# Stage one of a Fourier-mixing kernel: partner rows brought together through DRAM and added on GpSimd

## The chip, the cores and the metric

One core of a Trainium2 chip. The time is device microseconds of one execution of the whole program. Engines are named as the profile names them: PE (TensorE, matrix products; PEld is its weight load), DVE (VectorE), ACT (ScalarE), POOL (GpSimd) and SP (SyncE, which here issues DMA transfers). Sixteen DMA engines move data between DRAM and on-chip memory.

## The reference

```
x: (8, 3072, 256) float32, w1, w2, w3: (256, 768), w_out: (768, 256)
X   = real(fft(fft(x, axis=1), axis=2))         # per batch, 3072 x 256
t   = X.reshape(24576, 256)
h   = max(max(t @ w1, t @ w2), t @ w3)
out = h @ w_out                                  # (24576, 256) float32
```

## The kernel before

The two Fourier transforms are done as matrix products, and the product with w1, w2 and w3 is folded into the second transform's matrices (`gE`, `gO`, `gD`), so that the feed-forward part reads only two half-spectra `tE` and `tO` per batch.

A sequence of 3072 rows is written as 24 x 128, and the 256 columns as four groups `g` of 64. In on-chip memory a batch stands as 96 partitions (4 groups times 24 rows `a`), with 128 rows `bb` and 64 columns `dl` along the free dimension. x is loaded in four chunks `ch` of 32 rows `bb` (33 for the overlap) into tiles `xs` of 96 x 33 x 64 fp32: `load_chunk` (L123) issues on SP's queue four transfers of 24 partitions each (`load_rows`, L107), in pieces of 256 bytes, and for the last chunk five small ones of the row that follows (`load_next`, L119).

Since x is real, column d of a batch pairs with column 64 - d of another group, with reversed rows. `turn_chunk` (L144) on GpSimd therefore writes two bf16 copies of each batch from 1 on into `x0`: a forward one, transposed to d-major (L155), and a reversed one (`reverse`, L158). Batches 2 to 7 have each chunk in four parts, two forward and two reversed. Stage one, `Mix.s(k, x0)` (L487), takes five columns d per call (three in the last). For each d it runs two matmuls into one PSUM region, the forward copy by `m24f` (L496) and the reversed one by `m24r` (L498). A call's result is evicted to `z` by ACT (L503, L506, L507). Stage two, `Mix.k(q)` (L522, L524), multiplies `z` by the table `tabs` into `t`.

The feed-forward part of a batch has three blocks of six units, 18 units (`UNITS`) in all. A unit runs `unit_plus` (L542, L543), `unit_out` (a relu on ACT, L556, and a max on DVE, L557) and the `unit_minus` (L550) of the unit before, and then some steps of the output part (`l2_some`), taken from a queue. Per block there are four output lines ("slots"), twelve per batch. A slot goes through these engines:

- `l2_odd`: PE L591 into a bank `po` (two of them), DVE L594 (`other`), then POOL L597, which adds `even` and `other`;
- twelve matmuls of `l2_hidden` (PE L567) into the same bank;
- `l2_block`: DVE L617 adds `po` and the line that L597 completed, into `ot` (six buffers); POOL L620 stores half of it with an indirect DMA, and SP L630 the other half.

All engines run in the order in which the program was written down; nothing is reordered. That order is laid out by hand in `plan`: `at(b, unit, fn)` puts a step of work behind the given unit of batch b. Stage one and two of batch b + 1 go in from unit `begin[b]` on: `s0` to `s6`, then `k0` to `k5`. `turn_chunk` of batch b + 2 goes into units 6 to 21 of batch b (11 to 21 in batch 0), one part a unit, and the loads (`fetch`, L775) of batch b + 3 go into units 18, 19, 20 and 22 of batch b. Before the loop, a first section builds the tables and takes batch 0 through stage one.

Of the kernel before, what the change touches and what calls it, by code (L numbers as in the profile page):

```python
# [33 lines left out]
def kernel(  # L34
# [9 lines left out]
    nc = tc.nc  # L44

    B, S, D = x.shape
    assert (S, D) == (3072, 256)
    DFF = moe_w1.shape[1]
# [3 lines left out]
    UNITS = 3 * NJC  # L52
# [7 lines left out]
    consts = ctx.enter_context(tc.tile_pool(name="consts", bufs=1))  # L60
    ps_f = ctx.enter_context(tc.tile_pool(name="ps_f", bufs=2, space=bass.MemoryType.PSUM))
    xs_pool = ctx.enter_context(tc.tile_pool(name="xs", bufs=4))
    x0_pool = ctx.enter_context(tc.tile_pool(name="x0", bufs=2))
    t_pool = ctx.enter_context(tc.tile_pool(name="tbuf", bufs=2))

    m24f = consts.tile([96, 96], BF16, tag="m24f")
# [68 lines left out]
    def reverse(copy, xr, xs, r0, n, d0=32, d1=65):  # L135

        last = r0 + n > 128
        for (lo, hi, m) in ((d0, min(d1, 64), n), (64, d1, n - 1)) if last else ((d0, d1, n),):
            if lo < hi:
                copy(out=xr[:, lo - 32:hi - 32, 129 - r0 - m:129 - r0],  # L140
                     in_=bass.AP(xs.tensor, xs.offset + (m - 1) * 64 + lo,
                                 [xs.ap[0], [1, hi - lo], [-64, m]]))

    def turn_chunk(b, ch, part=None):  # L144

        if (b, "v") not in turned:
            x0 = x0_pool.tile([96, 66 * 130], BF16, name="x0", tag="x0")
            v = x0.rearrange("p (dl bb) -> p dl bb", bb=130)
            turned[b] = (lambda d: v[:, d, 0:128], rows_back(v[:, 33:66, :]))
            turned[b, "v"] = v  # L150
        v = turned[b, "v"]
        xs = raw[b, ch]
        for (d0, d1) in (((0, 17), (17, 33))[part % 2:part % 2 + 1] if part is not None else ((0, 33),)):
            if part is None or part < 2:
                nc.gpsimd.tensor_copy(v[:, d0:d1, ch * 32:ch * 32 + 32],  # L155
                                      xs[:, 0:32 * 64].rearrange("p (bb dl) -> p dl bb", dl=64)[:, d0:d1, :])
            if part is None or part >= 2:
                reverse(lambda out, in_: nc.gpsimd.tensor_copy(out, in_), v[:, 33:66, :], xs,  # L158
                        ch * 32, 33 if ch == 3 else 32, 32 + d0, 32 + d1)

    def signed():
        nc.scalar.activation(out=gw[:, 514:770], in_=gw[:, 256:512], func=AX.Copy, scale=sgn)
# [17 lines left out]
    def rows_back(v):  # L180
        return lambda d: v[:, 32 - d, 0:128] if d else v[:, 32, 1:129]

    raw_w = [consts.tile([128, 2 * DFF], FP32, name=f"raw_w{i}", tag=f"raw_w{i}") for i in (2, 3)]

    def cols(t, jh):
        return t.rearrange("p (fc j) -> p fc j", fc=2)[:, :, jh * 384:(jh + 1) * 384]
# [12 lines left out]
        nc.gpsimd.iota(t, pattern, base=base, channel_multiplier=cm,  # L199
                       allow_small_or_imprecise_dtypes=True)  # L200

    x0_first = x0_pool.tile([96, 64 * 130], BF16, name="x0", tag="x0")
    x0v = x0_first.rearrange("p (bb dl) -> p bb dl", dl=64)
    xs_a = xs_pool.tile([96, 33 * 64], FP32, name="xs", tag="xs")
    rows_a = xs_a.rearrange("p (bb dl) -> p bb dl", dl=64)
    load_rows((nc.sync, nc.sync, nc.scalar, nc.scalar), rows_a[:, 0:16, :], 0, 112, 128)
# [56 lines left out]
    turn = 2.0 * math.pi  # L263
# [34 lines left out]
    for (r0, r1) in ((0, 3), (3, 7)):  # L298
# [5 lines left out]
                          in_=up[:, 0:13].unsqueeze(1).to_broadcast([96, 2, 13]))  # L304
# [105 lines left out]
    for ch in range(4):  # L410
# [11 lines left out]
                        in_=moe_w_out.rearrange("(jc p) c -> p jc c", jc=NJC))  # L422
# [56 lines left out]
    class Mix:  # L479
# [7 lines left out]
        def s(self, k, x0, pool=ps_f, evict=nc.scalar.copy):  # L487

            ps1 = pool.tile([128, 512], FP32, name="ps1", tag="ps")
            if k < len(DLS):  # L490
                parts = [(d, 96, m24f, m24r) for d in range(*DLS[k])]
            else:
                parts = [(0, 52, m0f, m0r), (32, 48, m24f, m24r), (1, 96, m24f, m24r)]
            c0 = 0
            for (d, n, mf, mr) in parts:
                nc.tensor.matmul(ps1[:, c0:c0 + n], x0[0](d), mf[:, 0:n],  # L496
                                 start=True, stop=False)
                nc.tensor.matmul(ps1[:, c0:c0 + n], x0[1](d), mr[:, 0:n],  # L498
                                 start=False, stop=True)
                c0 += n  # L500
            if k < len(DLS):
                lo = 4 * DLS[k][0]
                evict(out=z[:, lo:lo + 20, 0:24],  # L503
                      in_=ps1[:, 0:480].rearrange("p (c r) -> p c r", r=24))
            else:
                evict(out=z_all[:, 0:52], in_=ps1[:, 0:52])  # L506
                evict(out=z[:, 2:8, 0:24],  # L507
                      in_=ps1[:, 52:196].rearrange("p (c r) -> p c r", r=24))
# [266 lines left out]
    def fetch(b, ch):  # L775
        raw[b, ch] = load_chunk(b, ch)
# [1 line left out]
    ahead = (("s0",), ("s1",), ("s2",), ("s3",), ("s4",), ("s5",), ("s6",),  # L778
             ("k0",), ("k1",), ("k2",), ("k3",), ("k4",), ("k5", "end"))
    first_ahead = (11, 12, 13, 13, 14, 14, 15, 16, 16, 17, 18, 19, 20)  # L780
    begin = [11, 6] + [5] * (B - 3)

    def l2_first():
        for _ in l2_even(0, 0):
# [3 lines left out]
    for (u, fn) in ((0, prep_some), (0, prep_some), (0, lambda: tab_sines(7, 10, (2,))),  # L788
                    (1, prep_some), (1, prep_some), (1, prep_some),
                    (2, lambda: m.k(2)), (2, prep_some), (2, lambda: tab_sines(10, 13, (0,))),  # L790
                    (3, prep_some), (3, lambda: tab_sines(10, 13, (1, 2))),
                    (4, lambda: m.k(3)), (4, prep_some), (5, prep_some), (5, l2_first),
                    (6, lambda: m.k(4)), (7, lambda: m.k(5)), (7, m.end),
                    (0, lambda: turn_chunk(1, 0)), (2, lambda: tab_minus(10, 13, nc.gpsimd)),
                    (2, lambda: turn_chunk(1, 1)),
                    (5, lambda: turn_chunk(1, 2)),
                    (7, lambda: turn_last(0)), (8, lambda: turn_last(1)),
                    (8, lambda: lay_last(0)), (9, lambda: lay_last(1)), (20, signed)):
        at(0, u, fn)
    for ch in range(4):  # L800
        at(0, (6, 7, 9, 11)[ch], lambda ch=ch: fetch(2, ch))
    for b in range(B - 1):
        for i, whats in enumerate(ahead):
            for what in whats:
                at(b, begin[b] + i if b else first_ahead[i], lambda b=b, what=what: piece(b + 1, what))
        if b + 2 < B:
            for ch in range(4):
                for part in range(4):
                    at(b, 6 + 4 * ch + part if b else 11 + 11 * (4 * ch + part) // 16,
                       lambda b=b, ch=ch, part=part: turn_chunk(b + 2, ch, part))  # L810
                if b + 3 < B:
                    at(b, UNITS + (0, 1, 2, 4 if b else 6)[ch], lambda b=b, ch=ch: fetch(b + 3, ch))

    for b in range(B):
        mm = mixes[b]
# [76 lines left out]
```

## Time and profile before

| | |
|---|---|
| median of 3 runs | 412.85 us (412.58 to 413.83) |
| the profiled execution | 412.57 us, its span 410.8 us |
| TensorE clock granted | 1.0 in all slices |
| PE busy | 393.8 us, 3018 matmuls |
| POOL busy | 319.8 us |
| DMA | 52.70 MB, mean 128 GB/s |

How to read it: the profile is of one execution. A group line names the source line, engine, operation, tiles with shape and type, count, then busy time, mean duration in ns and the idle time in front of it with what ended it. Queue q1 in the page's list is SP's DMA queue, q0 that of GpSimd. The "chain" follows the work that ended last back to the start.

### The profile page before, as it was taken

The page shows a single profiled execution, that of the slowest core. Times are in us where ns is not written, and L with a number is a line of the kernel's source. Part 1 is how long each engine was busy: PE and PEld are TensorE (multiplying, and loading weights), DVE is VectorE, ACT ScalarE, POOL GpSimd, SP SyncE. Part 2 cuts the span into 40 slices and gives each one's busy share as a digit, 9 for nine tenths or more (in the row PEclk, how much of TensorE's full clock was granted, in tenths as well). Part 3 has the DMA queues.
Part 4 walks back from the last instruction along what each step waited for, and adds up shares of the span by engine and source line. Part 5 has one row for each costly group of instructions (what it writes and reads, how often), then busy time and mean ns, then how long its engine had stood idle before and what let it go on. Part 6 is the DMA issues. An engine that isn't in the chain of part 4 may idle for free.

```text
span 410.8 us, 9043 instructions
## 1 busy us (share of the span) xinstructions
PE 393.8 (96%) x3018; PEld 268.9 (65%) x3072; DVE 308.8 (75%) x556; ACT 266.6 (65%) x489; POOL 319.8 (78%) x428
## 2 busy tenths in 40 slices
PE   0999999999999999999999999999999999999996
PEld 0465667766676677667676667667666666766665
DVE  8798767776768776786777777787668767778884
ACT  6787776767666667657765666656775676655550
POOL 9598999998888888889789798888878844446651
PEclk9999999999999999999999999999999999999999
DMA  9989895784228841586217852387411221211314
GB/s 116 194 173 180 179 234 148 183 205 111 81 87 207 172 136 53 140 211 141 100 65 188 190 137 88 94 208 151 124 65 67 65 76 67 79 53 51 107 65 142
DMA packets 131111, 52.70 MB, mean 128 GB/s; under 512 B 113009, under 2 KB 128120, under 8 KB 131064
## 3 DMA queue, kind: packets, MB, share of 16 engines
q1 hardware_dynamic: 106496, 37.50, 37.4%
q0 software_dynamic: 23632, 14.29, 15.7%
q8 instruction: 24, 0.39, 0.4%
q10 hardware_dynamic: 936, 0.33, 0.3%
q14 instruction: 23, 0.19, 0.2%
HBM read 29.02 MB, written 25.17 MB: 132 GB/s over the span
## 4 chain that ended last, share of the span: by engine, by line
PE 92%; POOL 3%; DVE 2%; issue 1%; DMA 1%; ACT 0%; DVEq 0%; ACTq 0%; POOLq 0%
PE po L567 31%; PE pse L542 16%; PE pse L550 15%; PE pse L543 13%; PE po L591 3%; PE ps L496 3%; PE ps L522 3%; POOL x L107 3%; PE ps L498 3%; PE ps L524 3%; PE pl L580 2%; DMA x<-in_x_dram 1%; PE psg L436 1%; DVE hm L557 1%; PE psw L465 0%
## 5 line engine op out<-in xcount | busy, mean ns | idle before, releaser
L556 ACT ACTIVATE stmp<-pse 128x512 bf16<-128x512 f32 x288 | 171.5, 600 | 44.9 <-PE pse L543 31.2
L557 DVE TENSOR_TENSOR hp<-pse,stmp 128x512 bf16<-128x512 f32 x144 | 99.4, 691 | 87.2 <-ACT stmp L556 64.5
L620 POOL DMA_INDIRECT out_dram<-ot,rows_m x92 | 102.6, 1115 | 53.2 <-DVE ot L617 41.3
L542 PE MATMUL pse<-t,gE 128*128 128x512 bf16 x288 | 109.2, 379 | 2.2
L557 DVE TENSOR_TENSOR hm<-pse,stmp 128x512 bf16<-128x512 f32 x144 | 99.1, 688 | 3.8 <-ACT stmp L556 3.5
L543 PE MATMUL pse<-t,gO 128*128 128x512 bf16 x249 | 94.3, 379 | 0.0
L567 PE MATMUL po<-wout_bf,hp 128*128 128x256 bf16 x576 | 85.9, 273 | 0.0
L567 PE MATMUL po<-wout_bf,hm 128*128 128x256 bf16 x570 | 85.3, 273 | 0.1
L597 POOL TENSOR_TENSOR even<-even,other 128x256 f32<-128x256 f32 x92 | 66.4, 722 | 21.9 <-DVE other L594 19.6
L550 PE MATMUL pse<-t,gD 128*128 128x512 bf16 x273 | 82.4, 379 | 0.7
L567 PEld LDWEIGHTS <-hp 128*128 128x128 bf16 x576 | 56.3, 98 | 17.1 <-issue 1.9
L567 PEld LDWEIGHTS <-hm 128*128 128x128 bf16 x576 | 56.3, 98 | 16.6
L617 DVE TENSOR_TENSOR ot<-po,even 128x512 f32<-128x512 f32 x92 | 62.7, 681 | 0.0
L158 POOL CAST x<-xs 96x544 bf16<-96x544 f32 (+5 forms) x57 | 60.5, 1068 | 0.0
L155 POOL CAST x<-xs 96x544 bf16<-96x544 f32 (+2 forms) x51 | 58.8, 1156 | 1.4 <-DMA xs<-in_x_dram 1.4
L526 ACT CAST t<-ps 128x512 bf16<-128x512 f32 x48 | 27.9, 585 | 34.5 <-PE ps L524 34.4
L550 PEld LDWEIGHTS <-gD 128*128 128x128 bf16 x288 | 27.9, 98 | 32.2
L503 ACT CAST z_all<-ps 128x480 bf16<-128x480 f32 x46 | 25.4, 559 | 33.5 <-PE ps L498 33.5
L594 DVE SCALAR_TENSOR_TENSOR other<-twice,po 128x256 f32<-128x256 f32 x92 | 43.7, 475 | 0.1
L543 PEld LDWEIGHTS <-gO 128*128 128x128 bf16 x288 | 28.1, 98 | 20.3 <-issue 2.0
L542 PEld LDWEIGHTS <-gE 128*128 128x128 bf16 x288 | 28.1, 98 | 19.6 <-issue 0.7
L583 ACT COPY even<-pl 128x512 f32<-128x512 f32 x46 | 27.0, 587 | 10.1 <-PE pl L580 9.7
(171 smaller groups left out, 382.9 us busy)
## 6 DMA issues: line engine op xcount, KB each, us to landing
xs<-in_x_dram SPq DMA_DIRECT2D x84, 198.0 KB
out_dram<-ot SPq DMA_DIRECT2D x90, 128.0 KB
xs<-in_x_dram SPq DMA_DIRECT2D x28, 192.0 KB
raw_w<-in_moe_w_dram SPq DMA_DIRECT2D x4, 384.0 KB
out_dram<-ot,rows_m POOLq DMA_INDIRECT x92, 3.6
out_dram<-ot SPq DMA_DIRECT2D x17, 64.0 KB
x<-in_x_dram POOLq DMA_DIRECT2D x8, 120.0 KB, 6.3
xs<-in_x_dram SPq DMA_DIRECT2D x32, 5.8 KB
```

Source lines behind the costliest of these rows:

```text
L155: nc.gpsimd.tensor_copy(v[:, d0:d1, ch * 32:ch * 32 + 32], xs[:, 0:32 * 64].rearrange("p (bb dl) -> p dl bb", dl=64)[:, d0:d1, :])
L158: reverse(lambda out, in_: nc.gpsimd.tensor_copy(out, in_), v[:, 33:66, :], xs, ch * 32, 33 if ch == 3 else 32, 32 + d0, 32 + d1)
L542: nc.tensor.matmul(pse[:, 0:n], gE[i][:, js], te, start=True, stop=False)
L543: nc.tensor.matmul(pse[:, 0:n], gO[i][:, js], to, start=False, stop=True)
L550: nc.tensor.matmul(pse, gD[i][:, js], to, start=False, stop=True, skip_group_check=True)
L556: nc.scalar.activation(out=stmp[:, 0:n], in_=pses[0][:, 0:n], func=AX.Relu)
L557: nc.vector.tensor_tensor(out=dst, in0=src3, in1=stmp[:, 0:n], op=ALU.max)
L567: nc.tensor.matmul(po, hcols(jc), wout_bf[:, jc * 256:(jc + 1) * 256], start=False, stop=(jc == NJC - 1), skip_group_check=True)
L594: nc.vector.scalar_tensor_tensor(out=other, in0=twice, scalar=po[:, 256:257], in1=po[:, 0:256], op0=ALU.mult, op1=ALU.subtract)
L597: nc.gpsimd.tensor_tensor(out=line[:, 256:512], in0=line[:, 0:256], in1=other, op=ALU.add)
L617: nc.vector.tensor_tensor(out=ot, in0=po, in1=lin, op=ALU.add)
L620: stored(nc.gpsimd.indirect_dma_start(out, bass.IndirectOffsetOnAxis(ap=rows_m[0:128 - lo, b * 12 + slot: b * 12 + slot + 1], axis=0), ot[ ...
```

## The change

For batches 2 to 7 the two bf16 copies are replaced by one folded copy `xw` of 34 x 128. Each chunk `xs` is sent as it is, fp32, to a DRAM buffer `held`, with the four groups in reversed order (`send_chunk`, four transfers of 24 partitions with 8,448 bytes in each), and read back from there into `xp` with the 24 rows of each group in reversed order (`fetch_turned`, one transfer of 96 partitions). So `xp` has in each partition the rows that pair with those of `xs`. `fold_chunk` adds the two on GpSimd in fp32, reading `xp` reversed, for d = 1 to 32 (in two parts of 16 columns), and writes bf16. Two small copies per chunk fill the columns 0 and 33. `Mix.s` then runs one matmul by `m24f` for each d from 1 to 32, and two for d = 0. Batches 0 and 1 stay as they were.

Chunks are taken in pairs, (1, 2) and (0, 3), since chunk `ch` needs the partner of chunk `3 - ch`. The loads come in the order 1, 2, 0, 3, from units 18, 19, 21 and 23. In batch b from 1 on, the first pair of batch b + 2 is sent at units 6 and 7, fetched at 8 and 9 and added at 10 to 13; the second is sent at 9 and 10, fetched at 14 and 15 and added at 16 to 19. Stage one of batch 2 begins at unit 8 of batch 1, and no longer at 6. To make room, `x0` has one buffer, and the fp32 weights `raw_w` share the two buffers of `xp`.

```diff
-    x0_pool = ctx.enter_context(tc.tile_pool(name="x0", bufs=2))
+    x0_pool = ctx.enter_context(tc.tile_pool(name="x0", bufs=1))
+    xp_pool = ctx.enter_context(tc.tile_pool(name="xp", bufs=2))
+    xw_pool = ctx.enter_context(tc.tile_pool(name="xw", bufs=2))
+    turn_pool = ctx.enter_context(tc.tile_pool(name="turn", bufs=4, space=bass.MemoryType.DRAM))
...
+    def send_chunk(b, ch):
+        xs = raw[b, ch]
+        held = turn_pool.tile([4, 24 * 33 * 64], FP32, name="held", tag="held")
+        for g in range(4):
+            nc.sync.dma_start(out=held[3 - g].rearrange("(a r) -> a r", a=24),
+                              in_=xs[g * 24:(g + 1) * 24])
+        sent[b, ch] = held
+
+    def fetch_turned(b, ch):
+        held = sent[b, ch]
+        xp = xp_pool.tile([128, 33 * 64], FP32, name="xp", tag="xp")[0:96]
+        n = 33 * 64
+        nc.sync.dma_start(out=xp, in_=bass.AP(held.tensor, held.offset + 23 * n,
+                                              [[24 * n, 4], [-n, 24], [1, n]]))
+        partner[b, ch] = xp
+
+    def fold_chunk(b, ch, part):
+        if b not in turned:
+            xw = xw_pool.tile([96, 34 * 128 + 16], BF16, name="xw", tag="xw")
+            turned[b] = xw[:, 0:34 * 128].rearrange("p (dl bb) -> p dl bb", bb=128)
+        v = turned[b]
+        bb = slice(ch * 32, ch * 32 + 32)
+        xs, xo, xp = raw[b, ch], raw[b, 3 - ch], partner[b, 3 - ch]
+        d0, d1 = ((1, 17), (17, 33))[part]
+        nc.gpsimd.tensor_tensor(
+            out=v[:, d0:d1, bb],
+            in0=xs[:, 0:32 * 64].rearrange("p (bb dl) -> p dl bb", dl=64)[:, d0:d1, :],
+            in1=bass.AP(xp.tensor, xp.offset + 33 * 64 - d0, [xp.ap[0], [-1, d1 - d0], [-64, 32]]),
+            op=ALU.add)
+        if part:
+            nc.gpsimd.tensor_copy(v[:, 33, bb], bass.AP(xo.tensor, xo.offset + 32 * 64,
+                                                        [xo.ap[0], [-64, 32]]))
+        else:
+            nc.gpsimd.tensor_copy(v[:, 0, bb], xs[:, 0:32 * 64:64])
...
-    raw_w = [consts.tile([128, 2 * DFF], FP32, name=f"raw_w{i}", tag=f"raw_w{i}") for i in (2, 3)]
+    raw_w = [xp_pool.tile([128, 33 * 64], FP32, name="xp", tag="xp")[:, 0:2 * DFF] for i in (2, 3)]
...
             for (d, n, mf, mr) in parts:
-                nc.tensor.matmul(ps1[:, c0:c0 + n], x0[0](d), mf[:, 0:n],
-                                 start=True, stop=False)
-                nc.tensor.matmul(ps1[:, c0:c0 + n], x0[1](d), mr[:, 0:n],
-                                 start=False, stop=True)
+                if isinstance(x0, tuple):
+                    pairs = ((x0[0](d), mf), (x0[1](d), mr))
+                else:
+                    pairs = ((x0[:, d, :], mf),) if d else ((x0[:, 0, :], mf), (x0[:, 33, :], mr))
+                for i, (st, mv) in enumerate(pairs):
+                    nc.tensor.matmul(ps1[:, c0:c0 + n], st, mv[:, 0:n], start=(i == 0),
+                                     stop=(i == len(pairs) - 1))
...
-    begin = [11, 6] + [5] * (B - 3)
+    begin = [11, 8] + [5] * (B - 3)
...
         if b + 2 < B:
-            for ch in range(4):
-                for part in range(4):
-                    at(b, 6 + 4 * ch + part if b else 11 + 11 * (4 * ch + part) // 16,
-                       lambda b=b, ch=ch, part=part: turn_chunk(b + 2, ch, part))
+            for pair, out_at, back_at, fold_at in (
+                    ((1, 2), *(((6, 7), (8, 9), (10, 11, 12, 13)) if b else
+                               ((11, 12), (13, 13), (15, 16, 17, 17)))),
+                    ((0, 3), *(((9, 10), (14, 15), (16, 17, 18, 19)) if b else
+                               ((14, 15), (17, 18), (20, 21, 22, 22))))):
+                for i in range(4):
+                    at(b, fold_at[i], lambda b=b, ch=pair[i % 2], part=i // 2:
+                       fold_chunk(b + 2, ch, part))
+                for i in range(2):
+                    at(b, out_at[i], lambda b=b, ch=pair[i]: send_chunk(b + 2, ch))
+                    at(b, back_at[i], lambda b=b, ch=pair[i]: fetch_turned(b + 2, ch))
```

More of the change, by code (lines that the diff above doesn't have):

```diff
@@ L142, in reverse, with turn_chunk @@
                                  [xs.ap[0], [1, hi - lo], [-64, m]]))
-    def turn_chunk(b, ch, part=None):
+    def turn_chunk(b, ch):
         if (b, "v") not in turned:
-            x0 = x0_pool.tile([96, 66 * 130], BF16, name="x0", tag="x0")
-            v = x0.rearrange("p (dl bb) -> p dl bb", bb=130)
+            x0 = x0_pool.tile([96, 68 * 128], BF16, name="x0", tag="x0")
+            v = x0[:, 0:66 * 130].rearrange("p (dl bb) -> p dl bb", bb=130)
             turned[b] = (lambda d: v[:, d, 0:128], rows_back(v[:, 33:66, :]))
@@ L152, in turn_chunk @@
         xs = raw[b, ch]
[L153 to L159, printed above, removed]
+        nc.gpsimd.tensor_copy(v[:, 0:33, ch * 32:ch * 32 + 32],
+                              xs[:, 0:32 * 64].rearrange("p (bb dl) -> p dl bb", dl=64)[:, 0:33, :])
@@ new lines, in turn_chunk @@
+        reverse(lambda out, in_: nc.gpsimd.tensor_copy(out, in_), v[:, 33:66, :], xs,
+                ch * 32, 33 if ch == 3 else 32)
+    sent = {}
+    partner = {}
+    def send_chunk(b, ch):
[12 more added lines that the diff above has]
+        partner[b, ch] = xp
@@ L200, in iota @@
                        allow_small_or_imprecise_dtypes=True)
-    x0_first = x0_pool.tile([96, 64 * 130], BF16, name="x0", tag="x0")
-    x0v = x0_first.rearrange("p (bb dl) -> p bb dl", dl=64)
+    x0_first = x0_pool.tile([96, 68 * 128], BF16, name="x0", tag="x0")
+    x0v = x0_first[:, 0:64 * 128].rearrange("p (bb dl) -> p bb dl", dl=64)
     xs_a = xs_pool.tile([96, 33 * 64], FP32, name="xs", tag="xs")
@@ L800 @@
     for ch in range(4):
-        at(0, (6, 7, 9, 11)[ch], lambda ch=ch: fetch(2, ch))
+        at(0, (6, 7, 9, 11)[ch], lambda ch=ch: fetch(2, (1, 2, 0, 3)[ch]))
     for b in range(B - 1):
@@ L806 @@
         if b + 2 < B:
-            for ch in range(4):
-                for part in range(4):
-                    at(b, 6 + 4 * ch + part if b else 11 + 11 * (4 * ch + part) // 16,
-                       lambda b=b, ch=ch, part=part: turn_chunk(b + 2, ch, part))
-                if b + 3 < B:
-                    at(b, UNITS + (0, 1, 2, 4 if b else 6)[ch], lambda b=b, ch=ch: fetch(b + 3, ch))
+            for pair, out_at, back_at, fold_at in (
[9 more added lines that the diff above has]
+                    at(b, back_at[i], lambda b=b, ch=pair[i]: fetch_turned(b + 2, ch))
+            if b + 3 < B:
+                for ch in range(4):
+                    at(b, UNITS + ((0, 1, 3, 5) if b else (0, 1, 5, 6))[ch],
+                       lambda b=b, ch=ch: fetch(b + 3, (1, 2, 0, 3)[ch]))
     for b in range(B):
```

## The prediction

> **What bounds the kernel now.** I read the page first, then the windows of steady batches, then TensorE's groups and one stretch of its timeline, then GpSimd against VectorE, and the DMA queues last. Page, busy times and chain:
>
> ```profile
> PE 393.8 (96%) x3018; PEld 268.9 (65%) x3072; DVE 308.8 (75%) x556; ACT 266.6 (65%) x489; POOL 319.8 (78%) x428
> PE 92%; POOL 3%; DVE 2%; issue 1%; DMA 1%; ACT 0%; DVEq 0%; ACTq 0%; POOLq 0%
> ```
>
> TensorE carries 92% of the chain. Three whole batches, from one first eviction of stage one to the next (columns: stretch, length, busy time and count by engine, clock, DMA share of 16 engines, GB/s):
>
> ```profile
> 134.60:181.80 47.20, 46.83 (x364) 32.50 (x370) 35.41 (x61) 31.01 (x57) 40.09 (x53) 1.00 0.53 136
> 181.80:229.00 47.20, 46.83 (x364) 32.38 (x369) 35.29 (x61) 31.01 (x57) 40.03 (x53) 1.00 0.52 136
> 229.00:276.20 47.20, 46.83 (x367) 32.45 (x371) 35.41 (x61) 30.96 (x57) 40.05 (x53) 1.00 0.54 137
> ```
>
> A batch is 47.20 us, 99% of it TensorE; a unit, its eighteenth, is 2.62 us. What is taken off TensorE comes off the time, as long as nothing else takes over the period. GpSimd (40.1) and the DMA engines (0.53 x 16 x 47.2 = 400 engine-us) have room on average. The 0.53 is not even, as the stretch with x loads shows beside the one after it (same columns):
>
> ```profile
> 169.00:188.00 19.00, 18.89 (x147) 12.72 (x147) 15.04 (x26) 11.67 (x21) 16.42 (x23) 1.00 0.89 206
> 188.00:216.00 28.00, 27.79 (x218) 19.57 (x221) 20.17 (x35) 19.10 (x37) 23.37 (x32) 1.00 0.29 91
> ```
>
> **TensorE's saving.** Timeline of one `s` piece, ten matmuls:
>
> ```profile
> 53.31 0.21 PE L496 MATMUL ps<-m24f,x 96*128 96x96 bf16 x1
> 53.36 0.20 PE L498 MATMUL ps<-m24r,x 96*128 96x96 bf16 x1
> ...
> 53.74 0.38 PE L542 MATMUL pse<-t,gE 128*128 128x512 bf16 x1
> ```
>
> Ten take 53.74 - 53.31 = 0.43 us, 0.043 each (0.2 is latency). The change drops 32 of 66 per batch (one each for d = 1 to 32): 32 x 0.043 = 1.4 us, a little less for the one of 48 columns; call it 1.35, and for six batches 8.1 us. The profiled execution took 412.57 us (span 410.8), the median of the runs is 412.85; so TensorE alone would give 412.6 - 8.1 = 404.5.
>
> **GpSimd.** Rows by form:
>
> ```profile
> L155 POOL CAST x<-xs 96x544 bf16<-96x544 f32 x24 | 27.2, 1133 | 0.0
> L155 POOL CAST x<-xs 96x512 bf16<-96x512 f32 x24 | 25.7, 1073 | 0.0
> L597 POOL TENSOR_TENSOR even<-even,other 128x256 f32<-128x256 f32 x92 | 66.4, 722 | 21.9 <-DVE other L594 19.6 <-ACT z_all L507 2.2
> L158 POOL CAST x<-xs 96x32 bf16<-96x32 f32 x6 | 1.4, 227 | 0.0
> ```
>
> Removed: 16 casts a batch, with L158's other forms (27.2 + 25.7 + 20.7 + 19.5 + 7.0 + 6.3 + 1.4)/6 = 18.0 us. Added: eight adds of 512 and eight copies of 32. An add is bounded below by the contiguous adds (256 in 0.722, 384 at L281 in 1.005, so 512 in 1.29) and above by two strided reads at the casts' 2 ns an element, 2.1; with the copies at 0.23, 12.2 to 18.6 us. GpSimd's sum stays or falls: nothing on the path by itself. But each add now waits for a DMA, and behind it in GpSimd's order stand L597 and the indirect store L620.
>
> **What those waits do.** A pair's fetches are put at units 8 and 9 (second pair 14, 15), and SP holds them back to back. The first add needs the second fetch, and is put at unit 10 (16), 2.6 us later. Cover on GpSimd and VectorE:
>
> ```profile
> 209.60 0.72 POOL L597 TENSOR_TENSOR even<-even,other 128x256 f32<-128x256 f32 x1
> 214.57 0.68 DVE L617 TENSOR_TENSOR ot<-po,even 128x512 f32<-128x512 f32 x1
> ```
>
> L597 at 209.60 serves the L617 at 214.57, and follows a cast directly; so a held add has some 4.3 us before L617 stands, and VectorE with it, and 1 to 2 more until TensorE has no free `pse` bank: 6 us in all.
>
> **DMA, the disputed cost.** Queues and sizes of before:
>
> ```profile
> q1 hardware_dynamic: 106496, 37.50, 37.4%
> q0 software_dynamic: 23632, 14.29, 15.7%
> xs<-in_x_dram SPq DMA_DIRECT2D x84, 198.0 KB
> out_dram<-ot,rows_m POOLq DMA_INDIRECT x92, 3.6
> ```
>
> From the trace's packet records, mean time: 256 B 19.4 ns, 1 KB 48.8, 4 KB 172, 8 KB (instruction fetch) 429 median and 307 at least. A row of 8,448 B is then 317 to 442 ns; I take 330, by the quick 8 KB ones and the 4 KB rate (355).
>
> How many engines share a transfer? q1's transfers move 89,568 rows of 256 B, 12,679 of 1 KB and 1,024 of 1.5 KB: 103,271. The other 3,225 packets are the 4-byte end marks, one for each engine used. They come out exactly with 16 marks for transfers of 128 or 64 rows (111 of them), 12 for 24 rows (114), 4 for 4 rows (8), 1 for 23 rows (32), 9 and 8 for the two odd stores: 1,776 + 1,368 + 32 + 32 + 17. So a transfer uses the largest number up to 16 that divides its rows. In all of these both sides count alike. The fetch does not: 96 partitions, from a pattern of 4 groups of 24 rows. Bounds: 16 engines by its target, 4 by its source's outer count. I take 4, nearest to the 4-row transfers, since 4 is the count that both sides can be cut by. Which four no view names; I take the same four each time, and price the rest as a rival.
>
> The Trainium skill, page "DMA: Bandwidth & Descriptors", section "Why a DMA increments its semaphore by 16 and not by 1", has a rule that speaks against this change: a transfer issued from SP takes the largest number of engines up to 16 that divides the slowest count of both sides, the lowest-numbered ones. By that rule the sum is the 555 below, and without it 434; the trace agrees for equal counts by the 3,225 marks, and no run so far shows unequal ones.
>
> On four engines a fetch is 24 rows x 0.33 = 7.9 us, a pair 15.8. Busiest engine, per batch:
> - x loads, 12,672 rows over 12 engines x 19.4 ns: 20.5 us
> - stores, direct (96 x 48.8 ns) and indirect with their small packets: 11.6
> - sends, 16 transfers of 24 rows, 2 rows an engine x 0.33: 10.6
> - fetches, 4 x 7.9: 31.7
>
> Together 74.4 us, where before it was 32 and where TensorE needs 45.9. That is one end of the new period. The other is TensorE with the waits: landing 15.8 + some 3 (L620 lands after 3.6), less 2.6 until GpSimd comes and less 6 of cover, is 10 us of standing per pair: 45.9 + 20 = 66. Both act, for a fetch also queues behind loads and sends on its engines; I take 71. Six bodies (0 to 5) hold such work: 412.6 + 6 x (71 - 47.2) = 555.
>
> Unknown ends: rows at 317 ns and loads at their peak (about 205 GB/s, 15 ns a packet) give 64 by waits, 514 us in all; rows at 442 ns give 89, or 663. TensorE after standing: its first matmuls after 9.6 us of idleness came 0.40 us apart instead of 0.22 for 2.4 us, so some 1.3 us each of twelve times, partly under the DMA; it belongs to the upper half.
>
> **Edits that cost nothing.** `begin` of batch 2 moves two units; its `t` for blk 0 (k0, k1 at units 15, 16) is still ahead of unit 18. Twenty more issues on SP, 0.33 to 0.98 us each, 7 to 20 us: SP mostly waits for L617. Stores held behind a fetch: six `ot` buffers last 23 us. `raw_w` in `xp`'s buffers and the single `x0`: both are free before the first fetch, and before batch 1's casts.
>
> **Rivals.**
> - A, faster: fetches on 16 engines (7.9 us a batch) and loads at peak (15.7): 15.7 + 11.6 + 10.6 + 7.9 = 45.8, just under TensorE's 45.9, and a fetch lands in some 5 us, inside the cover. 404.5 us. The point is the engine count: the busiest engine's fetches must fall from 31.7 to about 8. For: 96 target rows. Against: no transfer here used more engines than both of its sides' counts divide by.
> - B, spread but full: the same spread, or pairs on different fours, with loads at their mean 19.4: 50.6 a batch, +3.4 x 6, so 433 to 434. Slower, by the sends and loads on the same twelve engines (0.89 busy in load stretches).
> - C, little change: the saving and a short GpSimd wait cancel, around 412.
>
> That fewer matmuls run is certain: 192 of them leave the program.
>
> **How the numbers follow.** Main case 0.80, A 0.06, B 0.10, C 0.02, beyond 650 another 0.02. The forecast is the main case's 555; it takes most of 475 to 650, which leaves out A, B, C and the tail, 0.2. A measurement of this kernel can tell some 0.3% (1.2 us) from no change. Faster 0.06, same 0.02, slower 0.92.
>
> **What would show it.** Right: a batch period near 71 us; GpSimd's longest waits for DMA at the adds, over 10 us, twice a batch; TensorE below 75% busy in bodies 0 to 5 and full after; end marks on q1 of 4 a fetch; 10 matmuls to 5 a piece. Wrong: 16 marks a fetch, adds near 1.3 us that wait for nothing, and a period of 46 us; or POOL busy rather than waiting, if an add takes over 3 us.

## The result, and the profile after

The changed kernel takes 651.25 us (median of 4 runs, 648.20 to 652.61), the kernel before 413.09 us in the same comparison: a ratio of 1.575, 95% interval 1.572 to 1.578. The profiled execution took 651.54 us, its span 649.8. The direction of the forecast holds, and so does the path that it described; its size (555, range 475 to 650) is too small. Ratios here and below are of the runs within 1.5% of a kernel's fastest, which all four of these are.

The page after, busy times, the clock by slices, SP's DMA queue and the chain by engine:

```profile
PE 417.0 (64%) x2880; PEld 270.9 (42%) x2880; DVE 309.5 (48%) x556; ACT 266.6 (41%) x489; POOL 316.4 (49%) x422
PEclk9999957788578896687975969959799568899999
q1 hardware_dynamic: 112352, 76.43, 42.7%
DMA 35%; PE 24%; POOL 16%; SPq 11%; issue 11%; DVE 3%; ACT 1%; POOLq 0%; ACTq 0%; DVEq 0%
```

TensorE has fallen from 92% of the chain to 24%; DMA, GpSimd and SP's issuing stand in its place. GpSimd's busy time hardly moved (319.8 to 316.4), so it waits and does not work longer. TensorE has 192 instructions fewer by the program, yet is busy longer: the clock it is granted falls to 0.5 in each of its long stands and stays there for another 2.7 to 5.9 us, in which its 512-column matmuls start 0.43 us apart and not 0.22. Three windows of about a batch each (columns as before: stretch, length, busy time and count of PE, PEld, DVE, ACT, POOL, clock, DMA share, GB/s):

```profile
138.40:223.00 84.60, 43.60 (x293) 28.33 (x292) 29.73 (x51) 26.97 (x50) 35.96 (x50) 0.78 0.52 147
223.00:307.00 84.00, 49.16 (x325) 31.70 (x324) 34.32 (x59) 31.12 (x57) 38.53 (x50) 0.78 0.53 150
307.00:391.00 84.00, 47.92 (x332) 31.73 (x332) 34.04 (x59) 29.37 (x55) 36.92 (x50) 0.80 0.54 153
```

The second and third are a little short of a batch: the first evictions of stage one come at 223.0, 308.3, 395.2, 480.2 and 563.8 us, so a batch takes 85.2 us in the mean where it took 47.2 (46.0 without the swap, by `no_swap` below), at the same DMA share (0.53). The share is an average over 16 engines: the DMA engines as a whole are busy for no larger part of the time, and it cannot show that four of them carry each fetch. The waits say who stands (engine and line, what it waited for: us in total, times, longest):

```profile
DVE ot L662 <- POOL even L642: 252.2, 34, 29.1
...
PE po L636 <- DVE ot L662: 218.3, 23, 28.5
POOL xw L191 <- DMA xp<-held: 180.6, 9, 32.0
```

Read from below it is the path that the prediction described: GpSimd stands at the add (L191) for the fetch, so L642 is late, so VectorE's L662 is late, so TensorE finds no free `po` bank (L636). Adding up all idle time ahead of GpSimd's adds, whatever releaser is named, gives 245.4 us: 165 at the six first pairs (27.5 each) and 80 at the six second ones (13.4 each).

One body on SP's queue and on GpSimd shows why the first pair is the worse one. SP (start, us, transfers):

```profile
229.06 4.69 SPq L122 DMA_DIRECT2D xs<-in_x_dram  x5
234.12 4.86 SPq L169 DMA_DIRECT2D held<-xs  x4
239.09 1.05 SPq L675 DMA_DIRECT2D out_dram<-ot  x1
240.19 4.01 SPq L169 DMA_DIRECT2D held<-xs  x4
244.30 0.52 SPq L675 DMA_DIRECT2D out_dram<-ot  x1
244.92 2.79 SPq L178 DMA_DIRECT2D xp<-held  x2
...
272.62 4.00 SPq L178 DMA_DIRECT2D xp<-held  x2
```

GpSimd in the same body, the first add of each pair (in brackets the idle time before it):

```profile
263.89 1.88 POOL L191 TENSOR_TENSOR xw<-xs,xp 96x512 bf16<-96x512 f32 x1 [26.31 <-DMA xp<-held]
...
293.25 1.88 POOL L191 TENSOR_TENSOR xw<-xs,xp 96x512 bf16<-96x512 f32 x1 [13.18 <-DMA xp<-held]
```

GpSimd is at the first add at 263.89 - 26.31 = 237.6, some seven us before SP begins to issue the fetches: the sends came late, behind the x loads and the five small transfers of L122, and SP stood 3 us among them until a chunk of x had landed. GpSimd then waits for the landing as well. At the second pair (293.25 - 13.18 = 280.1) the fetches are out 3.5 us ahead of it, and it waits for the landing alone. These fetches had to wait for the adds of the first pair, since `xp` has two buffers: the second of them goes out 4.0 us ahead of GpSimd in all six batches. From the second fetch's issue to the add it is 16 to 18 us in both.

### The profile page after: what moved, and what is told of

Its sections match the earlier page's. It is cut to its first block, busy times and chain, and to the rows that moved or that the text cites. A ratio compares the mean times of both kernels' runs of the same rounds, so it can differ in the third digit from the quotient of the medians.

```text
span 649.8 us, 8832 instructions
## 1 busy us (share of the span) xinstructions
PE 417.0 (64%) x2880; PEld 270.9 (42%) x2880; DVE 309.5 (48%) x556; ACT 266.6 (41%) x489; POOL 316.4 (49%) x422
## 3 DMA queue, kind: packets, MB, share of 16 engines
q1 hardware_dynamic: 112352, 76.43, 42.7%
## 4 chain that ended last, share of the span: by engine, by line
DMA 35%; PE 24%; POOL 16%; SPq 11%; issue 11%; DVE 3%; ACT 1%; POOLq 0%; ACTq 0%; DVEq 0%
DMA xp<-held 16%; DMA held<-xs 12%; PE po L612 8%; SPq L110 5%; POOL xw L191 5%; DMA xs<-in_x_dram 5%; PE pse L587 4%; POOL out_dram L665 4%; PE pse L588 4%; PE pse L595 4%; SPq L169 3%; POOL even L642 3%; DMA xp<-in_moe_w_dram 1%; SPq L122 1%; DVE ot L662 1%
## 5 line engine op out<-in xcount | busy, mean ns | idle before, releaser
L191 POOL TENSOR_TENSOR xw<-xs,xp 96x512 bf16<-96x512 f32 x48 | 92.9, 1935 | 245.4 <-DMA xp<-held 180.6
L662 DVE TENSOR_TENSOR ot<-po,even 128x512 f32<-128x512 f32 x92 | 63.1, 686 | 252.2 <-POOL even L642 252.2
L636 PE MATMUL po<-gw,t 128*128 128x257 bf16 x92 | 26.7, 290 | 218.5 <-DVE ot L662 218.3
L612 PEld LDWEIGHTS <-hp 128*128 128x128 bf16 x576 | 57.7, 100 | 240.9 <-issue 227.2
L587 PE MATMUL pse<-t,gE 128*128 128x512 bf16 x288 | 113.9, 396 | 0.8 <-DVE hm L602 0.2
L588 PE MATMUL pse<-t,gO 128*128 128x512 bf16 x288 | 113.1, 393 | 0.0
L612 PE MATMUL po<-wout_bf,hm 128*128 128x256 bf16 x570 | 93.3, 291 | 0.0
L612 PE MATMUL po<-wout_bf,hp 128*128 128x256 bf16 x576 | 89.9, 281 | 0.0
L595 PE MATMUL pse<-t,gD 128*128 128x512 bf16 x288 | 87.6, 386 | 0.0
L642 POOL TENSOR_TENSOR even<-even,other 128x256 f32<-128x256 f32 x92 | 66.5, 723 | 21.8 <-DVE other L639 21.8
L612 PEld LDWEIGHTS <-hm 128*128 128x128 bf16 x576 | 60.2, 105 | 20.4 <-issue 0.5
```

The lines of the kernel that those rows point to most:

```text
L191: nc.gpsimd.tensor_tensor(out=v[:, d0:d1, bb], in0=xs[:, 0:32 * 64].rearrange("p (bb dl) -> p dl bb", dl=64)[:, d0:d1, :], in1=bass.AP(xp. ...
L587: nc.tensor.matmul(pse[:, 0:n], gE[i][:, js], te, start=True, stop=False)
L588: nc.tensor.matmul(pse[:, 0:n], gO[i][:, js], to, start=False, stop=True)
L595: nc.tensor.matmul(pse, gD[i][:, js], to, start=False, stop=True, skip_group_check=True)
L612: nc.tensor.matmul(po, hcols(jc), wout_bf[:, jc * 256:(jc + 1) * 256], start=False, stop=(jc == NJC - 1), skip_group_check=True)
L642: nc.gpsimd.tensor_tensor(out=line[:, 256:512], in0=line[:, 0:256], in1=other, op=ALU.add)
```

## The experiments

**Theory 1**: the time is that of the kernel without a swap plus what GpSimd stands at the adds, and that is set by when the fetch goes out and by the few engines that carry it. **Theory 2**: the DMA work on the busiest engines sets the period, and the standing only shows it. Times are compared with `no_swap` (407.35 us); "stood" is all idle time ahead of the adds L191, from the trace.

**The change without the swap.** `send_chunk` returns at once and the partner is taken from the chunk at hand:

```diff
-        xs = raw[b, ch]
-        held = turn_pool.tile(...)
-        ...
+        return
...
-        nc.sync.dma_start(out=xp, in_=...)
-        partner[b, ch] = xp
+        partner[b, ch] = raw[b, ch]
```

> Neither sends nor fetches: each add reads the other chunk itself in place of its swapped copy, so the rows that are added are not the partner rows. What is left of the change is the saving of 192 matmuls and the eight adds a batch on GpSimd (1.94 us each in the changed kernel). Theory 1 (the changed kernel stands because of its transfers alone): GpSimd has 40.1 - 18.0 + 8 x (1.94 + 0.22) = 39.4 us a batch, less than TensorE's 45.9; 404 to 407 us. Rival (the adds hold up the output lines too): over 415 us.

407.35 us, ratio 0.987 (0.983 to 0.990). The page's busy times:

```profile
PE 386.5 (95%) x2832; PEld 260.8 (64%) x2880; DVE 309.0 (76%) x556; ACT 266.6 (66%) x489; POOL 318.5 (79%) x422
```

PE is busy 7.3 us less than before; GpSimd's adds wait for nothing. So the change without its swap is worth 5 to 6 us, no more, and all the rest, 244 us, belongs to the swap. In the spans it is the same: 649.8 - 405.5 = 244.3 us, of which TensorE is idle for 213.8 and busy for 30.5 (417.0 - 386.5).

**Only the sends.** As `no_swap`, with the sends kept and nothing fetched.

> The sends to DRAM stay, the fetches are left out, and each add reads the other chunk itself (not the partner rows). Theory 1: nobody waits for a send, the busiest DMA engine has 42.7 us a batch, under TensorE's 45.9: within 5 us of the kernel without any swap. Rival (sends and loads fill their twelve engines, and loads come late to the adds): 430 us or more.

432.04 us, ratio 1.044 (1.040 to 1.049): theory 1 missed here. The rival had the time right and the wait wrong, for no add waits for a load. Nothing waits for the sends either, yet they cost 25 us. VectorE shows where (waits):

```profile
DVE ot L657 <- DMA out_dram<-ot: 18.7, 8, 3.3
```

Its six `ot` buffers come free late, since the stores land late; the kernel before has no such wait. A row of 8,448 bytes took 467 ns on average here. Whether the stores are late on the DMA engines, which the sends use too, or already in SP's queue, which has 96 issues more, no run parts.

**Only the fetches.** The sends left out, the fetch in the same pattern but from x:

```diff
-        nc.sync.dma_start(out=xp, in_=bass.AP(held.tensor, held.offset + 23 * n,
+        nc.sync.dma_start(out=xp, in_=bass.AP(x.tensor, x[b].offset + (23 + 96 * (ch % 3)) * n,
                                               [[24 * n, 4], [-n, 24], [1, n]]))
```

> The fetches stay in shape and place, but read rows of x itself, and the sends are left out (the rows that are added are not the partner rows). Theory 1 (the first pair's stand of 27 us was the 16 of the fetches and 11 of sends that came late): both pairs now hold GpSimd some 14 us and TensorE 11.5, a batch is 45.9 + 23 + 4 for the slower clock = 73, in all about 570 us. Theory 2 (the four engines of the fetches are full all the time and set the period): 20.5 + 11.6 + 31.7 = 64 a batch, about 512 us.

610.48 us; stood 204 us, and the time is 203 above `no_swap`. That is above what either theory gave, and two lines of the trace tell why (SP's queue, then GpSimd):

```profile
221.95 1.37 SPq L172 DMA_DIRECT2D xp<-in_x_dram  x2
```
```profile
240.37 1.88 POOL L185 TENSOR_TENSOR xw<-xs,xp 96x512 bf16<-96x512 f32 x1 [18.33 <-DMA xp<-in_x_dram]
```

The fetch is issued at 221.95, GpSimd arrives at 240.37 - 18.33 = 222.04. Two units lie between them in the plan and no time on the chip: both engines had been waiting for the same output line (SP for its store, GpSimd for its own, L659), and were released together. In the six first pairs the second fetch went out 0.4 to 7.3 us behind GpSimd, 2.6 in the mean.

**Fetches on 16 and on 8 engines.** The same bytes, sends and places, another pattern:

```diff
-        ... held.offset + 23 * n, [[24 * n, 4], [-n, 24], [1, n]]
+        ... held.offset + 5 * n,  [[6 * n, 16], [-n, 6], [1, n]]     # fetch_16
+        ... held.offset + 11 * n, [[12 * n, 8], [-n, 12], [1, n]]    # fetch_8
```

> Sends as in the changed kernel, the fetch cut as 16 groups of 6 rows, reversed within each group (so the rows that are added are not the partner rows; bytes and transfers are the same). If the count of engines follows the outer count of both sides, each fetch leaves 16 end marks, not 4, and a pair takes 4 us, not 15.8. Theory 1: the first pair still stands 27 - 11.5 = 15 us on GpSimd, 11 on TensorE, the second nothing; 45.9 + 11 + 2 = 59 a batch, about 483 us. Theory 2: the busiest engine has 50.6 us a batch, about 434 us. If the fetch stays on four engines: 651 us.

530.30 us, stood 125 (110 of it at first pairs), 123 above `no_swap`.

> As the fetch on 16 engines, but in 8 groups of 12 rows (not the partner rows), so 8 marks a fetch and 12 rows on each engine: a pair takes 7.7 us, between 3.8 (16 engines, 530 us) and 15.4 (four, 651). Theory 1 (the time is GpSimd's standing, and it stands as long as the fetches take, twice a batch): 3.85 us more than on 16 engines, twelve times, 530 + 46 = 576 us. Theory 2 (busiest engine's work): 58 us a batch against 50.6, 530 + 44 = 574; this run alone does not part them, it tests the price of a microsecond of fetch. Rival (the four engines are the trouble as such): near 530.

557.84 us, stood 152.5 (121 and 31), 150.5 above. The end marks are 16 and 8 a fetch. From the second fetch's issue to the add it is 17.0, 9.6 and 7.0 us in the mean with 4, 8 and 16 engines, and the second pair stands 13, 5 and 2.5 us. The first pair falls to 18 only on 16 engines, for 10.9 of that is the late send: so much behind GpSimd's arrival goes its second fetch out. Theory 1 had the cause and not the sizes: 483 and 576 were foretold, 47 too low and 18 too high. Theory 2 gave 434 for 16 engines and falls: the work is spread, and the time is 96 us above that.

**The same work earlier.** In the first, the fetch of the first pair in the kernel without sends; in the second, the sends and fetches of the whole change, with the loads of the second pair later:

```diff
-  ((1, 2), *(((6, 7), (8, 9), (10, 11, 12, 13)) if b else
+  ((1, 2), *(((6, 7), (5, 6), (10, 11, 12, 13)) if b else      # fetch_only_early
+  ((1, 2), *(((3, 4), (5, 6), (10, 11, 12, 13)) if b else      # early_sends
-  ((0, 3), *(((9, 10), (14, 15), (16, 17, 18, 19)) if b else
+  ((0, 3), *(((11, 12), (14, 15), (16, 17, 18, 19)) if b else  # early_sends
-                    at(b, UNITS + ((0, 1, 3, 5) if b else (0, 1, 5, 6))[ch],
+                    at(b, UNITS + (0, 1, 6, 8)[ch],                 # early_sends
```

> The kernel without sends (610 us, not the partner rows) with the first pair's fetches put at units 5 and 6 instead of 8 and 9, ahead of two more output lines. Theory 1 (a fetch put behind an output line's store on SP, and an add put behind the same line's store on GpSimd, are released by the same VectorE add, so the two units between them give no lead): the first pair's stand falls from 18 us by the two lines, some 8 us, less what the fetches now queue behind the last loads: 5 to 8 us a batch, 562 to 580 us. Theory 2 (engines 0 to 3 set the period by the amount of their work): within 10 us of 610.

594.08 us, stood 189, 187 above.

> The changed kernel, with all its work, resequenced: the first pair's sends at units 3 and 4 and its fetches at 5 and 6, the second pair's loads at 6 and 8 after them, its sends at 11 and 12. Theory 1 (late sends and no lead): the first pair's stand falls from 27 us to 12 to 17, the second stays near 14 or grows by a few us since its loads are later; 560 to 600 us. Theory 2 (amount of work on the busiest engines): within 15 us of 651.

644.53 us, stood 239, 237 above. Both took longer than theory 1 said, and `early_sends` lies where theory 2 had put it (within 15 us of 651): three units earlier in the plan won 2 us a first pair in the one and 5 in the other, and in `early_sends` the second pairs lost 23 us (from 80 to 104) of the 29 that the first ones won, when their loads and sends had been put later. Its first fetch did go out early, but x loads stood between the two fetches, and in five of six batches the second followed 15 to 20 us later; the issue of one of these loads alone held SP for 11.24 us (at 227.91). In all six kernels that fetch rows of 8,448 bytes, the time is 407 us plus GpSimd's standing, to within 2.4 us.

**A quarter of the bytes.** Only columns 32 to 63 are needed from the partner, and bf16 is enough for them. ScalarE packs each chunk into `xq`, and that is sent and fetched, a quarter of the bytes:

```diff
+        xq = xq_pool.tile([96, 33 * 32], BF16, name="xq", tag="xq")
+        nc.scalar.copy(out=xq..., in_=xs.rearrange("p (bb dl) -> p bb dl", dl=64)[:, :, 32:64])
-                              in_=xs[g * 24:(g + 1) * 24])
+                              in_=xq[g * 24:(g + 1) * 24])
```

> All the work is done, with a quarter of the bytes: ScalarE packs the 32 columns that the adds read into bf16 (96 x 1056, some 2 us at the rate of its 96x528 row, four times a batch), rows of 2,112 bytes go to DRAM and back, xp has four buffers, first pair sent at units 4 and 5 and fetched at 6 and 7, second sent at 8 and 10 and fetched at 11 and 12. Both theories: a fetch pair on four engines takes 48 x 0.09 = 4.3 us, the busiest engine 20.5 + 11.6 + 2.9 + 8.6 = 43.6 a batch, GpSimd waits little: 405 to 425 us. Rival (ScalarE's packing, 8 us a batch between the relus, holds up TensorE): 430 us or more.

475.43 us, ratio 1.152 (1.149 to 1.156), where both theories had said 405 to 425; stood 54, all at first pairs, 68 above. Then with more lead: adds later, four `xq` buffers, and the sends issued by ScalarE or by SP:

> All the work is done. As the packed kernel (475 us: GpSimd stood 52 us, all at first pairs, and relus on ScalarE waited for packing buffers), with four packing buffers, the sends issued from ScalarE's queue right behind the packing, so that no load on SP stands between, and the adds put three to four units behind the fetches (first pair: packed at units 5 and 7, fetched at 9, added at 12 to 15; second: 9 and 11, 13, 17 to 20; in body 0 fetched at 14, 15 and 17, 18). Theory 1 (time = 407 us + GpSimd's standing, a microsecond for a microsecond): a fetch lands some 7 us behind its issue and the lead is 8 to 10, so GpSimd stands less than 5 us in all; 407 to 415 us. Rival (packing and sends on ScalarE stand between the relus): ScalarE's waits for loads or buffers grow over 15 us, 420 us or more.

> The same with the sends back on SP's queue. Theory 1: what counts is when a fetch lands, not who issues it; SP's loads of the second pair stand ahead of the second send of the first pair and make the fetch up to 10 us later; GpSimd stands 0 to 5 us per first pair, 407 to 440 us, and 407 plus the standing that the trace shows.

494.38 us, ratio 1.197 (1.194 to 1.200), and 469.64, ratio 1.136 (1.134 to 1.139). In the first GpSimd stands 10 us in all, and the kernel is the slowest of the three: theory 1 does not cover this one. ScalarE's groups and waits show work that the relus stand behind:

```profile
L169 ACT CAST xq<-xs 96x1056 bf16<-96x1056 f32 x24 | 25.7, 1072 | 9.7 <-DMA xs<-in_x_dram 9.7
```
```profile
ACT stmp L607 <- DMA held<-xq: 26.2, 14, 2.6
```

A cast of 1.07 us, and behind it four issues that hold ScalarE another 1.7 to 2.6 us, 24 times, while the relus of L607 wait. Casts, issues and the casts' waits for x add up to 80 us, where the excess less the standing is 77; that each of them reaches the time is argued from this sum. In the second, where SP issues, GpSimd stands 36 us, and the excess is 62.

**The cast alone.** `no_swap` with the 24 casts, into a tile that nobody reads:

```diff
-        return
+        xs = raw[b, ch]
+        xq = xq_pool.tile([96, 33 * 32], BF16, name="xq", tag="xq")
+        nc.scalar.copy(out=xq..., in_=...[:, :, 32:64])
```

> The kernel without the swap (407.35 us: the adds take the other chunk's rows, nothing is sent or fetched), and in addition ScalarE packs each chunk's 32 columns to bf16 as in the packed kernels, into a tile that nobody reads: 24 casts of 1.07 us. What the packed kernels lost beyond GpSimd's standing is said by theory 1 to be this cast, standing between two relus that TensorE waits for: up to 25.7 us more, 425 to 433. The rival: ScalarE is busy 66% of the time and takes the casts in its gaps, 407 to 412; the loss then belongs to the sends.

442.17 us in the median of four runs from 436.01 to 446.00. The traced run is the fastest, 29 us above `no_swap`, the next is 33 above: more than the 25.8 us that the casts take. In the trace some of them also wait, mostly for their x loads (14.5 us in all, `ACT xq`). ScalarE was busy 66% and the casts were not hidden at all. The smaller rows were bought with an engine whose delay TensorE feels.

**The swap ahead of time, from DRAM to DRAM.** No engine packs or sends. x itself is copied into `held` a batch ahead, 32 columns, groups and rows reversed, and fetched as 96 plain rows:

```diff
-    def send_chunk(b, ch):
-        ...
+    def mirror(b, i):
+        ...
+        def move(to, frm, dims):
+            nc.sync.dma_start(out=bass.AP(held.tensor, held.offset + to, [d[1] for d in dims]),
+                              in_=bass.AP(x.tensor, x[b].offset + frm, [d[0] for d in dims]))
+        if i < 8:
+            g, h = i // 2, i % 2
+            move(g * 24 * r + h * 64 * 32, (23 * 128 + h * 64) * 256 + (3 - g) * 64 + 32,
+                 [([256, 64], [32, 64]), ([-128 * 256, 24], [r, 24]), ([1, 32], [1, 32])])
...
-        nc.sync.dma_start(out=xp, in_=bass.AP(held.tensor, ...))
+        nc.sync.dma_start(out=xp, in_=held[:, ch * 32 * 32:(ch * 32 + 33) * 32])
```

> The whole swap is done from DRAM to DRAM ahead of time: x itself is copied into held with groups and rows reversed, 128-byte pieces of the needed 32 columns only, transfers of 64 x 24 pieces, a batch ahead of its use; then held is fetched as 96 plain rows of 4,224 bytes, five units before the adds. No engine sends anything. Theory 1 (time is 407 us and GpSimd's standing at the adds): 24 fetches with 16 end marks each, landing in a few us, no standing above 2 us, so 405 to 432 (the upper end by the 25 us that the sends cost by themselves in send_only). Theory 2 (the work on the busiest DMA engines sets the period): a batch adds 12,672 pieces; at the 19.4 ns of the 256-byte pieces that is 246 us of engine time over 16 engines, 15 each, and the fetches 384 rows x 0.172 / 16 = 4, on top of 32: 51 us a batch, 435 in all, more if a piece from DRAM to DRAM costs more than 19.4 ns.

470.94 us, ratio 1.140 (1.134 to 1.145), above what either theory gave (405 to 432, and 435); stood 65, and 407.35 + 65 = 472. The landing takes some 5 us, but the first pair's fetches still come late; SP's queue shows what they stood behind:

```profile
177.79 7.26 SPq L110 DMA_DIRECT2D xs<-in_x_dram  x2
185.10 2.43 SPq L122 DMA_DIRECT2D xs<-in_x_dram  x5
187.57 0.90 SPq L190 DMA_DIRECT2D xp<-held  x2
```

The last two kernels put the first pair's fetches ahead of those loads, at unit 17 of the batch before, and the second pair's five units earlier, and add batch 2 later; the second of them reverses the rows in the fetch again, in the change's pattern of 4 groups:

```diff
-  ((1, 2), *(((5, 6), (10, 11, 12, 13)) if b else ((11, 12), (15, 16, 17, 17)))),
+  ((1, 2), *(((-1, -1) if b > 1 else (4, 5), (10, 11, 12, 13)) if b else ((8, 10), (16, 17, 18, 19)))),
```

> As the copy from DRAM to DRAM, but with the lead made real: the first pair's fetches are issued at unit 17 of the batch before (from batch 4 on), ahead of the x loads on SP; batch 2 is added up to four units later. Theory 1 (407.35 us plus GpSimd's standing at the adds, which was 64 us there and made 471 of it): standing under 8 us, 405 to 416. The rival, that the added DMA work and the 60 more issues on SP set the time, and that standing is only where it shows: the standing moves to other waits (GpSimd's indirect stores, VectorE's L673 for stores), 440 or more.

> The same with the rows reversed by the fetch again, in the change's own pattern of 4 groups of 24 rows: 4 end marks a fetch, 24 rows of 4,224 bytes on each of four engines, some 4.3 us a fetch instead of 1.1. Theory 1: the few engines cost only through the time of landing, and the lead covers that: within 4 us of the run beside it. The rival, that four busy engines hold up the loads and stores that share them: 10 us or more above it.

The first gave 465.56 us in the median of eight runs between 457.77 and 470.62; the ratio, 1.111 (1.108 to 1.113), is of the three fastest (median 459.48), and the traced run took 467.14, 8 us more than that. From batch 4 on GpSimd stands 0.3 us at the adds, and still a batch takes 54 us (its first adds at 183.0, 237.5, 291.6 and 345.3). Theory 1 (405 to 416) missed, the rival was right: the standing moved to the stores. Waits, and two lines of SP's queue:

```profile
PE po L647 <- DVE ot L673: 42.4, 20, 8.5
...
DVE ot L673 <- DMA out_dram<-ot: 34.8, 12, 6.6
```
```profile
274.23 6.32 SPq L110 DMA_DIRECT2D xs<-in_x_dram  x4
280.67 5.28 SPq L686 DMA_DIRECT2D out_dram<-ot  x1
```

One store takes 5.28 us to issue, and the next comes 10 us after it; DMA's share in these batches is 0.75 to 0.85. The second kernel gave 532.48, ratio 1.288 (1.286 to 1.290): 73 us above the 459.48, with the same plan. GpSimd stood 55 us in it and 24 in the first, so the adds account for some 30 of the 73. VectorE's wait for the stores, `DVE ot L675 <- DMA out_dram<-ot`, grew to 86.7 us, 20 times, and SP's queue shows why:

```profile
254.90 16.98 SPq L110 DMA_DIRECT2D xs<-in_x_dram  x4
```

These four x loads, right behind two fetches (issued from 253.43 on), hold SP for 17 us (6.32 in the first kernel, above), and the next store goes out behind them, at 271.97. GpSimd does not stand at the adds of these fetches (277.4), so a fetch on four engines holds up the stores even where nobody waits for the fetch, here by way of the queue that issues both; SP's issuing of x loads (L110) is 16% of this kernel's chain. Theory 1 is right for the change as it was made, and no law: once the lead is there, SP's queue and the crowding on the DMA engines are the next bound; for the kernel with 16 engines a fetch no run parts the two. None of the kernels that carry out the whole swap came near 413 us. The best that taking away the swap could give is 1.3%.

## Why the prediction was right or wrong

- **TensorE's saving**: 8.1 us foretold, 7.3 in busy time and 5.5 in time (`no_swap`).
- **Four engines a fetch**: held. q1's 112,352 packets hold 4,473 end marks: the 3,225 of before, 96 x 12 of the sends, 24 x 4 of the fetches. `fetch_16` and `fetch_8` follow the same count. By the rule of the Trainium skill that the prediction cited (page "DMA: Bandwidth & Descriptors", section "Why a DMA increments its semaphore by 16 and not by 1"), unequal counts on the two sides should do just that; the runs agree, with 4, 8 and 16 marks against 96 partitions.
- **A row of 8,448 bytes at 330 ns**: right for the fetches (348 on average in `fetch_only`, 319 in the median), short for the sends (467 on average in `send_only`). The landing was taken as 15.8 + 3 = 18.8 us and took 17.0 in the mean.
- **The lead of 2.6 us: a step that failed.** It counted the unit between the second fetch and the add in the plan as time. On the chip the second fetch went out 10.9 us behind GpSimd's arrival at first pairs and 4.0 ahead of it at second ones, a lead of -3.4 in the mean. At first pairs the two engines leave the same output line together (`fetch_only`: 221.95 and 222.04), and in the whole change the x loads, the five small ones and the eight sends precede the fetch on SP: 16.6 us in the body shown (3.05 of it four x loads from 225.95 on, the rest in the lines above). They were priced as DMA work, and SP's issues were put among the edits that cost nothing, at 0.33 to 0.98 us each; in the kernel before, 67 of SP's 267 issues already took over 1 us, the longest 5.63. At second pairs the fetch waits for `xp`'s buffers. So GpSimd stood 27.5 and 13.4 us, 20.4 in the mean, where the terms (15.8 + 3 - 2.6) gave 16.2.
- **The cover of 6 us a pair: the second step that failed.** TensorE's twelve long stands at L636 are 17.5 us each under GpSimd's 20.4: the cover was 2.9. VectorE stood 2.3 us less than GpSimd, where 4.3 had been read off a cast, and TensorE 0.6 less than VectorE; what it lacked was a `po` bank (L636), not a `pse` bank.
- **TensorE after standing: the term left out of the 66.** For 49.6 us of its busy time, behind the twelve stands, its clock was 0.5, and its matmuls were busy 30.5 us longer (417.0, where `no_swap` has 386.5). That is 2.5 us a pair and took back nearly all of the cover. The prediction had 1.3 and left it to the "upper half".
- **The sum.** In the four steady batches GpSimd stood 39.4 us a batch, where 32.4 had been counted: 7.0 more. The cover was 5.8 and not 12: 6.2 more. The longer matmuls added 5.1. From the 66 "by waits" that makes 84, where 85.2 was measured; and GpSimd's 245 us came through to the time in full (244 above `no_swap`).
- **The busiest engine's 74.4 us, and 71 as the middle**: the middle gave the work on the busiest engine a weight that no run bears out. `fetch_16` takes the fetches off those engines and still takes 530, so this work is not what set the period; what the four engines set is the landing. The low end is off by a little too: by its own terms "64 by waits" is 65.
- **The add**: 1.94 us, between the bounds of 1.29 and 2.1, beside no path.
- **Rivals**: A is what `no_swap` shows (404.5 foretold, 407.35), but 16 engines do not lead there. B's 434 is near `send_only` (432.04), where stores came late; that twelve full engines were the reason, as B has it, is not shown.
- **What would show it**: 4 marks, GpSimd's waits over 10 us twice a batch and TensorE under 75% busy (52 to 59% in the windows) came; a period near 71 did not, it was 85.

## What to carry to other kernels

A unit in a plan is not time: ask of two engines whether they are released by the same event, and count a lead only from one engine's last wait to the other's; then go through the issuing queue and add up all that stands ahead of the transfer. Here, with two `po` banks between them, a stand of GpSimd came through to TensorE nearly whole, and the slower clock after it took back the little cover that there was. When the wait is cured, look at the transfers themselves: their price (25 us for the sends here, for a saving of 6) was there all along, hidden under the standing.

## What the runs showed of the hardware

- Transfers that nobody waits for cost time through others: 96 sends of 198 KB each took 25 us, by `ot` buffers that came free late.
- An x load that SP issued within 5 us of a pair of fetches on four engines (rows of 8,448 bytes) held SP for 9.25 to 12.88 us, five times in the changed kernel; with rows of 4,224 bytes in `mirror_lead_4` it was up to 14.48. The longest issue of one transfer in the kernel before was 5.63 us, with sends alone 6.10, in `fetch_8` and `fetch_16` 5.05, in `mirror_lead` 6.44.
- In the changed kernel the granted clock was 0.5 at the end of each of TensorE's twelve long stands (9 to 29 us) and for 2.7 to 5.9 us more; matmuls of 512 columns started 0.43 us apart there, and 0.22 at 1.0.
- A cast of 1.07 us on an engine that is busy 66% was not hidden: 24 of them, with their waits for x loads, cost 29 and 33 us in the two faster runs.
- 73,728 pieces of 128 bytes from DRAM to DRAM took 13.2 ns each on average, those of 256 bytes into on-chip memory 19.2 in the same run (`mirror`).
